# Last tile of the second feed-forward layer: eight single blocks and four pairs instead of two and seven, part of the tile before it kept in weight slots, and another hand-written order

## The chip, the cores and the metric

One core of one Trainium2 chip. The metric is the device time of one execution in microseconds (us), as a median over runs. Beside the runs there is one profiled execution, from which all rows below come; its times are counted from the first instruction's start (the span).

## What is computed

Attention with squared ReLU, gated by `u`, feeds two feed-forward layers. The change touches the second layer alone:

```python
# first layer (ELU), then the second one:
h = x @ w_in                                  # 6016 tokens, 256 -> 2048
P = a[0] + a[1]*h + a[2]*h*h + a[3]*h*h*h
Q = 1.0 + abs(b[0])*abs(h) + abs(b[1])*h*h
g = P / (Q + 1e-06)
out = g @ w_out                               # 2048 -> 256
```

## The kernel before

Everything is held transposed: features on partitions, tokens along the free dimension. Each fp32 matmul is done as three fp32r matmuls (high weight by high data, low weight by high data, high weight by low data), so every operand exists as a high and a low part. The 6016 tokens are cut into 12 tiles, eleven of 512 and a last one of 384. Below, tile 10 is the next to last (`NFT - 2`) and tile 11 the last (`NFT - 1`); "512" is a block of tile 10, "384" one block of tile 11 and "768" two blocks of tile 11 side by side (a pair, in two neighbouring PSUM banks).

The hidden features are 16 blocks of 128. For each block the first layer runs `first_hidden` (six matmuls), `first_relu` and `first_exp` on ScalarE, `first_elu` on VectorE, `first_high` on ScalarE, `first_low` on GpSimd and `project` (six matmuls). The second layer runs `second_hidden` (six matmuls into one PSUM bank, or twelve into two for a pair), then the twelve steps that `second` lists, then `second_project`. Tile 11's second layer starts only when all of tile 11's first layer is projected and `x2_high` (ScalarE) and `x2_low` (VectorE) have split its sum; this moment is called the hand-over below.

The steps of `second` have two forms. Tile 10 and the tiles before it take the plain one: `linear` and `size` on ScalarE read the block from PSUM, `denominator`, `times` and `numerator` on VectorE each read it from PSUM once more, then `absolute`, `log` and `power` on ScalarE, `high`, `product` and `remainder` on VectorE with both tensor inputs in SBUF, and `rest` on GpSimd. Tile 11 takes another: `square`, `size`, `linear` on ScalarE; `cubic` (p = p times s) on GpSimd; `denominator` on VectorE as q = s times b1 plus q, with both inputs in SBUF; no `absolute`; `numerator` (written over the block in PSUM), `high` and `remainder` on VectorE with one input in PSUM; `product` with both in SBUF; `rest` on GpSimd. `groups` says how tile 11's 16 blocks are grouped: one single, seven pairs, one single.

SBUF slots: `wide()` takes one of 32 slots which held the split weights. A slot comes free when its last reader has run: the first layer's weights as tile 11 passes through the first layer, the second layer's as it passes through the second. Tile 11's p, s, q, r sit in such slots. The high and low parts of tile 10's result sit in the three slots of tag `x` (`second`, step `high`).

Up to tile 10's first layer the order is that of `ffn_step`. The rest (`finish`) is an order written out by hand: the string `LAST` lists the operations two characters each, `ROOM` the PSUM bank of each that opens one; an operation goes to its engine's queue in the order listed, and each queue is in order. An operation beyond the list is `warm_up`, a matmul whose result nobody reads, to keep TensorE's clock up.

Of the kernel before, what the change touches and what calls it, by code (L numbers as in the profile page):

```python
# [21 lines left out]
def attention_then_two_ffns(  # L22
# [63 lines left out]
    def sb2(tag, bufs, dt=F32R):  # L86
        return sp.tile([P, 2, W], dt, tag=tag, bufs=bufs, name=tag)
# [68 lines left out]
    V = {}  # L156
# [309 lines left out]
        if d == ND - 1:  # L466
            give_pair(("acc", 0, ti))

    groups = [1] + [2] * 7 + [1]

    def members(i):

# [15 lines left out]
    def second(i):  # L488

        last = i[0] == NFT - 1
        st, m, n = mid[i], len(members(i)), widths[i[0]]
        h = st["h"]
        v, act, tt, stt = nc.vector, nc.scalar.activation, nc.gpsimd.tensor_tensor, nc.vector.scalar_tensor_tensor

        def new(key, tag, bufs, dt=F32):  # L500
            t = wide(dt) if last else sb(tag, bufs, dt).rearrange("p (c w) -> p c w", c=1)
            st[key] = t[:, :m, :n]
            return st[key]

        def linear():
            act(new("p", "t", 3), h, AF.Identity, bias=a2, scale=a3)  # L506

        def square():
            act(new("s", "", 0), h, AF.Square)

        def size():
            act(new("q", "q", 4), h, AF.Abs, scale=b0 if last else b1)  # L512

        def cubic():
            tt(out=st["p"], in0=st["p"], in1=st["s"], op=ALU.mult)

        def denominator():
            if last:
                stt(out=st["q"], in0=st["s"], scalar=b1, in1=st["q"], op0=ALU.mult, op1=ALU.add)
            else:  # L520
                stt(out=st["q"], in0=st["q"], scalar=b0, in1=h, op0=ALU.add, op1=ALU.mult)  # L521

        def times():
            v.tensor_tensor(out=st["p"], in0=st["p"], in1=h, op=ALU.mult)  # L524

        def numerator():
            if last:
                stt(out=h, in0=h, scalar=a1, in1=st["p"], op0=ALU.mult, op1=ALU.add)  # L528
                st["top"] = h
            else:  # L530
                stt(out=st["p"], in0=st["p"], scalar=a1, in1=h, op0=ALU.add, op1=ALU.mult)
                st["top"] = st["p"]

        def absolute():
            act(st["q"], st["q"], AF.Abs)

        def log():
            act(new("r", "r", 2), st["q"], AF.Ln, bias=NQ * LNS, scale=LNS)

        def power():  # L540
            act(st["r"], st["r"], AF.Exp, bias=LNB, scale=-1.0)

        def high():
            if last:
                tag, bufs = ("rl", 4) if i[1] % 2 else ("x", 3)
                st["hi"], st["lo"] = (sb2(tag, bufs)[:, :m, :n] for _ in range(2))
            else:
                t = sb2("x", 3)
                st["hi"], st["lo"] = t[:, 0:1, :n], t[:, 1:2, :n]
            stt(out=st["hi"], in0=st["top"], scalar=a0, in1=st["r"], op0=ALU.add, op1=ALU.mult)  # L550
            g2[i] = st["hi"], st["lo"]

        def product():
            st["prod"] = st["s" if last else "q"]
            stt(out=st["prod"], in0=st["q"], scalar=NQ, in1=f(st["hi"]), op0=ALU.add, op1=ALU.mult)  # L555

        def remainder():
            stt(out=st["p"], in0=st["top"], scalar=a0, in1=st["prod"], op0=ALU.add, op1=ALU.subtract)  # L558

        def rest():  # L560

            eng = v if i == (NFT - 1, len(groups) - 1) else nc.gpsimd
            eng.tensor_tensor(out=st["lo"], in0=st["p"], in1=st["r"], op=ALU.mult)  # L563

        reads = {"remainder"} if last else {"linear", "size", "denominator", "times", "numerator"}

        def then_free(name, fn):
            def run():
                fn()
                if name in reads:  # L570
                    reads.remove(name)
                    if not reads:
                        (give_pair if m > 1 else give)(("h", 1, i))
            return run

        if last:
            steps = [
                ("square", "A", ["hidden"], square),
                ("size", "A", ["hidden"], size),
                ("linear", "A", ["hidden"], linear),  # L580
                ("denominator", "V", ["square", "size"], denominator),
                ("cubic", "G", ["square", "linear"], cubic),
                ("log", "A", ["denominator"], log),
                ("power", "A", ["log"], power),
                ("numerator", "V", ["cubic", "size"], numerator),
                ("high", "V", ["power", "numerator"], high),
                ("product", "V", ["high"], product),
                ("remainder", "V", ["product"], remainder),
                ("rest", "G", ["remainder"], rest),
            ]  # L590
        else:
            steps = [
                ("linear", "A", ["hidden"], linear),
                ("size", "A", ["hidden"], size),
                ("denominator", "V", ["size"], denominator),
                ("times", "V", ["linear"], times),
                ("numerator", "V", ["times"], numerator),
                ("absolute", "A", ["denominator"], absolute),
                ("log", "A", ["absolute"], log),
                ("power", "A", ["log"], power),  # L600
                ("high", "V", ["power", "numerator"], high),
                ("product", "V", ["high"], product),
                ("remainder", "V", ["product"], remainder),
                ("rest", "G", ["remainder"], rest),
            ]
        return [(name, eng, needs, then_free(name, fn)) for name, eng, needs, fn in steps]

    def second_step(i, name):
        ops = mid[i].setdefault("ops", {x[0]: x[-1] for x in second(i)})
        ops[name]()  # L610

    def second_project(i, parts=("high", "low"), b=None):
        project(1, i[0], members(i), g2[i], parts, b)
# [44 lines left out]
    def ffn_step(n):  # L658
# [42 lines left out]
            second_hidden(j)  # L701

    DIGITS = "0123456789abcdefghijklmnopqrstuvwxyzABCDEFGHIJKLMNOPQRSTUVWXYZ_-"
    ROOM = "21303012610312103412301201320331203102602460260111111111111111111111111"
    LAST = (
        "590e0r0d1e1a0405060G1f0H0g1c0I0f000h075h0i020t1b0j5i08090k010K0J0u1d0L1h0l5j0a0s5k5a0x0m5l0V1g1i0v0n5p0w"
        "0y0o0X0Y0b5b035x1l0c1m5c0z0A0p1j1k5m5q0M0B0C0W5y0Z5d5r5z1n5A0q5s5e0N5f0-0_5F0D0E0O0P1p1q101C5G0Q11125g5H"
        "0R135t5I0T1o1R1r5u0S1E1F1t5B1s5C1T14151u1v0F5N5O1I1w1U5n5P5Q1x1D241G5o5J5v1J1y1S1z261H1K271X0U1L5V5W1Y1Z"
        "5K1V1W1M165D175w5L2j5R5T1_5S5X192l1N1O18611A5Y2m2562281-692a1P292k2p1B6a20632n642o2b2c2d6b6c2y2A1Q2B225E"
        "21232q2r2e2s6d6e5M2f2E2g2t2z2C2N6h2P2Q6i2D5Z5_6j2h6k2F2u2G6p2T5U302H2I2J2i2O2R2K5-6q6r326l6m333f6s2v2S60"  # L710
        "3h31342w2U3i653u352V2W6x673g3j662x2X2L686f363l3J2Y2M3k3w3x6y3m3n3o6z6A2Z6g6F373p38396B3v3A3q6C6n3L3a3y6N"
        "2_3M3r6t3b3c6O6P6Q3K3N6o3B3d3C2-3z3P3Y6G6H3O3Q3D6v4b3_3E6V3e3R6I3F3-4d4e3Z3s71423S3H3t6u6w3G4h3I403T3U3V"
        "4c4f724i416J4g6D73746K4j4k4344454q6E6W6X4F4l4s6R6S464m47754n6Y6L4U4r486M4t4H3W4W6Z4u4X766T4v4G4J4w3X4x4I"
        "4y4z4L4M6_6-6U4K7770494A784B7b4o4a4p7c794V7a4Y7d4N4O4C4_4-7g507e7i4Z4P514Q4R7f7s7t7v527x7h53544D4S7u7j4E"
        "4T7w7k7H7y7z7I7J7K7M7l5556587A577m7B7n7o7p7L7N7W7O7Z7Y7q7r7C7D7E7P7Q897R7X8b7_807-7S7T7F827G8o8183847U7V"
        "8a8d8c8e858q8D8f8g8h868i8j878m8p8s8r8F8t8k8l8w8u8v8x8E8G888I8H8J8K8S8U8T8B8y8z8A8n958V8X8L8M9m9m8C8N8W8Y"
        "8Q8O8P8_8Z8-97909698999b9c9m9m9m9m9m9m9m9m9m9m9m9m9m8R919a929d9e9f9g939m9m9m9m9m9m9i949h9m9m9m9j9k9l"
    )
    BACK = 1

# [3 lines left out]
    def finish(n0):  # L724
# [12 lines left out]
        for ti in range(NFT):  # L737
# [23 lines left out]
            for g in range(len(groups) if ti == tl else NF):  # L761
                i = ti, g
                b = (ti + 1) * NF + LAG1 + members(i)[0]
                if b + LAG2 < n0:
                    continue
                if b >= n0:
                    mid[i] = {"h": None}
                    add(lambda at, i=i: second_hidden(i, at), True)
                for name, *_ in second(i):
                    if b + lags[name] >= n0:  # L770
                        add(lambda i=i, name=name: second_step(i, name))
                add(lambda at=None, i=i: second_project(i, ("high",), at), g == 0)
                add(lambda i=i: second_project(i, ("low",)))
            if b + LAG2 >= n0:
# [147 lines left out]
```

## Time and profile before

| | us |
|---|---|
| median of 3 runs (lowest, highest) | 1544.7 (1544.42, 1545.58) |
| the profiled execution, its own time | 1544.23 |
| its span, first to last instruction | 1542.4 |
| VectorE's `elu` of tile 10's last block starts (first VectorE operation of `LAST`) | 1386.27 |
| tile 11's hand-over: its first `x2_low` starts | 1476.67 |
| VectorE's last operation but the copy of the result: `rest` of tile 11's last block ends | 1537.94 |

The page gives busy time by engine over the whole span; the span cut into stretches says which engine is full where. Durations of back-to-back operations overlap a little, so the distance from one start to the next is shorter than the duration.

### The profile page before, as it was taken

The numbers are of one execution on the slowest core, as the hardware profiler recorded it, in microseconds if no ns is written. First come the engines' busy times: TensorE is split into PE (matmuls) and PEld (weight loads), VectorE is DVE, ScalarE is ACT, GpSimd is POOL, SyncE is SP. The second block draws the span as 40 slices with busy tenths as digits, with TensorE's granted clock in tenths as the row PEclk, the third lists the DMA queues.
The fourth block names the chain that finished last, engine by engine and source line by source line (L and its number), as shares of the span: only waits on it lengthen the run. The fifth ranks groups of instructions, "written<-read, shape, count | busy, mean of one in ns | idle before, by whom it ended". The sixth has DMA issues, their size and how long they took to land.

```text
span 1542.4 us, 24205 instructions
## 1 busy us (share of the span) xinstructions
PE 1521.5 (99%) x8898; PEld 1292.8 (84%) x8898; DVE 1395.9 (90%) x1848; ACT 1290.3 (84%) x1996; POOL 679.9 (44%) x531
## 2 busy tenths in 40 slices
PE   9999999999999999999999999999999999999987
PEld 7889999898888878888888888888888888888866
DVE  8999999999996689999999999999999999999998
ACT  7878776787776798989899998989888998989974
POOL 3344430343342444444444444444444444445565
PEclk9999999999999999999999999999999999999999
DMA  5343333222222400000000000000000000000000
GB/s 150 124 130 117 111 120 109 64 76 68 83 81 83 135 1 1 28 1 28 1 0 29 1 28 1 28 1 27 2 1 28 1 25 1 14 1 15 1 14 11
DMA packets 38423, 67.09 MB, mean 43 GB/s; under 512 B 5408, under 2 KB 14880, under 8 KB 38304
## 3 DMA queue, kind: packets, MB, share of 16 engines
q1 hardware_dynamic: 38144, 65.29, 13.0%
q8 instruction: 69, 1.13, 0.3%
q14 instruction: 50, 0.41, 0.1%
q10 hardware_dynamic: 160, 0.26, 0.1%
HBM read 45.88 MB, written 19.66 MB: 42 GB/s over the span
## 4 chain that ended last, share of the span: by engine, by line
PE 58%; DVE 5%; issue 2%; POOL 1%; ACT 1%; POOLq 0%; DVEq 0%; ACTq 0%
PE psum L423 10%; PE psum L403 10%; PE psum L402 10%; PE psum L405 10%; PE psum L420 10%; PE psum L421 10%; POOL hl L454 1%; DVE w L555 1%; DVE x L550 1%; DVE t L558 1%; DVE psum L528 0%; DVE w L558 0%; DVE q L555 0%; DVE q L521 0%; DVE t L524 0%
## 5 line engine op out<-in xcount | busy, mean ns | idle before, releaser
L563 POOL TENSOR_TENSOR x<-t,r 128x512 fp32r<-128x512 f32 x176 | 231.5, 1315 | 478.0 <-DVE t L558 377.6
L329 PE MATMUL psum<-hl,w 64*128 64x512 f32 (+1 forms) x2256 | 392.4, 383 | 0.0
L329 PEld LDWEIGHTS psum<-hl,w 64*128 64x128 f32 x2256 | 306.0, 184 | 29.3 <-DVE e L350 1.8
L329 PE MATMUL psum<-x,w 64*128 64x512 f32 (+1 forms) x1128 | 319.2, 382 | 0.0
L454 POOL TENSOR_TENSOR hl<-e,hl 128x512 fp32r<-128x512 f32 (+1 forms) x192 | 248.2, 1293 | 67.2 <-ACT hl L449 60.7
L292 ACT ACTIVATE w<-psum 128x1024 f32<-128x1024 f32 (+1 forms) x144 | 145.2, 1009 | 102.5 <-PE psum L290 99.9
L329 PEld LDWEIGHTS psum<-x,w 64*128 64x128 f32 x1128 | 194.5, 184 | 13.4
L506 ACT ACTIVATE t<-psum,coef 128x512 f32<-128x512 f32 x176 | 137.4, 781 | 71.6 <-PE psum L405 69.6
L293 DVE SCALAR_TENSOR_TENSOR psum<-psum,w 128x1024 f32<-128x1024 f32 (+1 forms) x144 | 173.5, 1205 | 21.4 <-ACT w L292 20.8
L305 DVE TENSOR_TENSOR x<-psum,hl 128x1024 fp32r<-128x1024 f32 (+1 forms) x144 | 173.1, 1202 | 14.6 <-ACT q L205 0.5
L521 DVE SCALAR_TENSOR_TENSOR q<-q,coef,psum 128x512 f32<-128x512 f32 x176 | 131.2, 746 | 59.6 <-ACT q L512 59.4
L402 PE MATMUL psum<-x,w 128*128 128x512 f32 (+1 forms) x384 | 148.9, 388 | 7.2 <-DVE w L558 7.2
L298 ACT ACTIVATE hl<-w 128x1024 fp32r<-128x1024 f32 (+1 forms) x144 | 150.6, 1046 | 4.2
L420 PE MATMUL psum<-hl,w 128*128 128x512 f32 (+1 forms) x384 | 147.9, 385 | 0.4 <-ACT hl L449 0.4
L403 PE MATMUL psum<-x,w 128*128 128x512 f32 (+1 forms) x384 | 148.2, 386 | 0.0
L402 PE MATMUL psum<-rl,w 128*128 128x512 f32 (+1 forms) x384 | 148.1, 386 | 0.0
L403 PE MATMUL psum<-rl,w 128*128 128x512 f32 (+1 forms) x384 | 147.8, 385 | 0.0
L421 PE MATMUL psum<-hl,w 128*128 128x512 f32 (+1 forms) x384 | 147.7, 385 | 0.0
L442 DVE SCALAR_TENSOR_TENSOR e<-e,psum 128x512 f32<-128x512 f32 (+1 forms) x192 | 128.5, 670 | 17.7 <-ACT e L438 17.4
L420 PE MATMUL psum<-x,w 128*128 128x512 f32 (+1 forms) x368 | 142.9, 388 | 0.0
L421 PE MATMUL psum<-x,w 128*128 128x512 f32 (+1 forms) x368 | 142.8, 388 | 0.0
L558 DVE SCALAR_TENSOR_TENSOR t<-t,coef,q 128x512 f32<-128x512 f32 x176 | 136.8, 778 | 5.7
(137 smaller groups left out, 3518.6 us busy)
## 6 DMA issues: line engine op xcount, KB each, us to landing
raw<-w_in_dram SPq DMA_DIRECT2D x16, 512.0 KB, 4.2
raw<-w_out_dram SPq DMA_DIRECT2D x16, 512.0 KB, 4.6
wd<-q SPq DMA_DIRECT2D x28, 256.0 KB, 2.3
raw<-wd SPq DMA_DIRECT2D x14, 512.0 KB, 3.4
raw<-v_dram SPq DMA_DIRECT2D x22, 256.0 KB, 4.2
outT_dram<-raw SPq DMA_DIRECT2D x22, 256.0 KB, 2.5
raw<-uT_dram SPq DMA_DIRECT2D x10, 512.0 KB, 5.0
xd<-raw SPq DMA_DIRECT2D x20, 256.0 KB, 2.4
```

The lines of the kernel that those rows point to most:

```text
L293: nc.vector.scalar_tensor_tensor(out=s, in0=s, scalar=SCALE, in1=e, op0=ALU.mult, op1=ALU.mult)
L305: nc.vector.tensor_tensor(out=lo[:, :, :w], in0=psum[:, i:i + 2, :w], in1=f(hi[:, :, :w]), op=ALU.subtract)
L329: nc.tensor.matmul(acc[ti][d, h][:, :w], lhsT=lhs[rows, j % 2, d * P:(d + 1) * P], rhs=rhs[rows, :w], start=j == 0 and k == 0, stop=k == 2 ...
L402: nc.tensor.matmul(h, lhsT=wh[:, d, c], rhs=x[d][0], start=d == 0, stop=False)
L403: nc.tensor.matmul(h, lhsT=wl[:, d, c], rhs=x[d][0], start=False, stop=False)
L405: nc.tensor.matmul(h, lhsT=wh[:, d, c], rhs=x[d][1], start=False, stop=d == ND - 1)
L420: nc.tensor.matmul(out, lhsT=wh, rhs=g[0][:, c], start=k == 0, stop=False)
L421: nc.tensor.matmul(out, lhsT=wl, rhs=g[0][:, c], start=False, stop=False)
L423: nc.tensor.matmul(out, lhsT=wh, rhs=g[1][:, c], start=False, stop=k == NF - 1)
L454: nc.gpsimd.tensor_tensor(out=lo[:, 0], in0=e, in1=f(hi[:, 0]), op=ALU.subtract)
L558: stt(out=st["p"], in0=st["top"], scalar=a0, in1=st["prod"], op0=ALU.add, op1=ALU.subtract)
L563: eng.tensor_tensor(out=st["lo"], in0=st["p"], in1=st["r"], op=ALU.mult)
```

## The change

It groups tile 11's 16 blocks as one single, four pairs, seven singles, each with a form. "signed" (the pairs): `square` and `cubic` as before, but `denominator` is the plain one, (q plus b0) times h, reading the block from PSUM, and `absolute` is added on ScalarE. "banks" (the singles): as before, but ScalarE's `size` writes its result into a free PSUM bank, `denominator` reads and writes that bank, and `log` and `product` read it; `product` then gives the bank back. Tile 10's blocks 2 to 15 write their high and low parts into `wide()` slots instead of tag `x`. `ROOM` and `LAST` are replaced.

```diff
-    groups = [1] + [2] * 7 + [1]
+    LAYOUT = ((1, "banks"), (2, "signed"), (2, "signed"), (2, "signed"), (2, "signed"), (1, "banks"), (1, "banks"), (1, "banks"), (1, "banks"), (1, "banks"), (1, "banks"), (1, "banks"))
+    groups = [n for n, _ in LAYOUT]
+    KEPT = 2
+    def kept(i):
+        return i[0] == NFT - 2 and i[1] >= KEPT
...
+        squared = form in ("cubic", "signed", "banks")
+        signed = form not in ("cubic", "banks")
...
-        def size():
-            act(new("q", "q", 4), h, AF.Abs, scale=b0 if last else b1)
+        def size(b=None):
+            if form == "banks":
+                bank(("q", 1, i), b)
+                b = banks_of["q", 1, i]
+                st["q"] = psum[:, b:b + 1, :n]
+            else:
+                new("q", "q", 4)
+            act(st["q"], h, AF.Abs, scale=b1 if signed else b0)
...
         def denominator():
-            if last:
+            if signed:
+                stt(out=st["q"], in0=st["q"], scalar=b0, in1=h, op0=ALU.add, op1=ALU.mult)
+            else:
                 stt(out=st["q"], in0=st["s"], scalar=b1, in1=st["q"], op0=ALU.mult, op1=ALU.add)
...
-                t = sb2("x", 3)
+                t = wide() if kept(i) else sb2("x", 3)
...
+                if name == "product" and form == "banks":
+                    give(("q", 1, i))
...
+        if signed:
+            steps += [("absolute", "A", ["denominator"], absolute)]
```

What the two `LAST` strings spell, counted by engine. TensorE's are matmuls, the others' operations, by the free size of one; "to the hand-over" ends before `x2_high`, the rest is "after":

| | before, to it | after it | changed, to it | after it |
|---|---|---|---|---|
| TensorE 512 / 384 | 244 / 192 | 26 / 216 | 206 / 192 | 64 / 200 |
| of the 384, warm-ups | 0 | 24 | 0 | 8 |
| VectorE 512 / 768 / 384 | 118 / 0 / 16 | 8 / 35 / 14 | 109 / 0 / 16 | 17 / 20 / 44 |
| ScalarE 512 / 768 / 384 | 103 / 0 / 48 | 7 / 35 / 13 | 97 / 0 / 48 | 13 / 24 / 43 |
| GpSimd 512 / 768 / 384 | 19 / 0 / 16 | 3 / 14 / 3 | 18 / 0 / 16 | 4 / 8 / 15 |

VectorE's 384 after the hand-over hold two `x2_low` and the copy of the result in both.

## Rows read from the trace of the kernel before

**Rows 1.** The page: busy time, share and instructions of each engine
```profile
PE 1521.5 (99%) x8898; PEld 1292.8 (84%) x8898; DVE 1395.9 (90%) x1848; ACT 1290.3 (84%) x1996; POOL 679.9 (44%) x531
```
**Rows 2.** Stretches: length, busy PE, PEld, DVE, ACT, POOL (instructions), PE clock, DMA, GB/s
```profile
1360.00:1380.00 20.00, 20.00 (x90) 16.56 (x89) 18.74 (x29) 17.65 (x30) 9.82 (x8) 1.00 0.00 1
...
1400.00:1420.00 20.00, 20.00 (x100) 17.78 (x99) 19.61 (x31) 18.49 (x37) 11.72 (x9) 1.00 0.00 1
...
1480.00:1500.00 20.00, 14.50 (x73) 12.36 (x72) 19.60 (x19) 14.57 (x21) 14.29 (x8) 1.00 0.07 27
1500.00:1520.00 20.00, 17.07 (x87) 16.10 (x86) 19.62 (x17) 12.73 (x17) 11.87 (x7) 0.91 0.00 1
1520.00:1540.00 20.00, 14.23 (x67) 12.63 (x65) 17.91 (x18) 7.68 (x12) 9.50 (x6) 0.91 0.00 2
```
**Rows 3.** VectorE in order of time: start, duration, operation
```profile
1386.27 0.68 DVE L442 SCALAR_TENSOR_TENSOR e<-e,psum 128x512 f32<-128x512 f32 x1
...
1470.14 0.73 DVE L521 SCALAR_TENSOR_TENSOR q<-q,coef,psum 128x512 f32<-128x512 f32 x1
1470.80 0.67 DVE L524 TENSOR_TENSOR t<-t,psum 128x512 f32<-128x512 f32 x1
...
1476.67 1.02 DVE L465 TENSOR_TENSOR x<-psum,x 128x384 fp32r<-128x384 f32 x2
...
1484.78 2.34 DVE L558 SCALAR_TENSOR_TENSOR t<-t,coef,q 128x512 f32<-128x512 f32 x1
...
1491.45 0.62 DVE L558 SCALAR_TENSOR_TENSOR w<-psum,coef,w 128x384 f32<-128x384 f32 x1
1491.98 1.01 DVE L519 SCALAR_TENSOR_TENSOR w<-w,coef 128x768 f32<-128x768 f32 x1
...
1505.93 2.58 DVE L519 SCALAR_TENSOR_TENSOR w<-w,coef 128x768 f32<-128x768 f32 x1
1508.44 1.01 DVE L558 SCALAR_TENSOR_TENSOR w<-psum,coef,w 128x768 f32<-128x768 f32 x1
1509.37 1.01 DVE L528 SCALAR_TENSOR_TENSOR psum<-psum,coef,w 128x768 f32<-128x768 f32 x1
...
1531.04 0.96 DVE L555 SCALAR_TENSOR_TENSOR w<-w,rl 128x768 f32<-128x768 f32 x1
```
**Rows 4.** GpSimd in order of time, beside VectorE's row at 1505.93
```profile
1505.44 2.25 POOL L515 TENSOR_TENSOR w<-w 128x768 f32<-128x768 f32 x1 [0.49 <-ACT w L506]
```
**Rows 5.** By line and form, 1385 to 1543: busy, mean ns, idle before it
```profile
L519 DVE SCALAR_TENSOR_TENSOR w<-w,coef 128x768 f32<-128x768 f32 x7 | 10.2, 1460 | 0.0
L555 DVE SCALAR_TENSOR_TENSOR w<-w,rl 128x768 f32<-128x768 f32 x4 | 7.1, 1782 | 0.1
L555 DVE SCALAR_TENSOR_TENSOR w<-w,x 128x768 f32<-128x768 f32 x3 | 5.9, 1961 | 0.1
L519 DVE SCALAR_TENSOR_TENSOR w<-w,coef 128x384 f32<-128x384 f32 x2 | 3.0, 1489 | 0.0
L528 DVE SCALAR_TENSOR_TENSOR psum<-psum,coef,w 128x384 f32<-128x384 f32 x2 | 1.2, 611 | 0.0
L506 ACT ACTIVATE w<-psum,coef 128x384 f32<-128x384 f32 x2 | 1.3, 664 | 0.0
L509 ACT ACTIVATE w<-psum 128x384 f32<-128x384 f32 x2 | 1.0, 477 | 0.0
```
**Rows 6.** TensorE in order of time, at either clock
```profile
1533.32 0.52 PE L420 MATMUL psum<-rl,w 128*128 128x384 f32 x1
1533.64 0.52 PE L421 MATMUL psum<-rl,w 128*128 128x384 f32 x1
...
1536.11 0.33 PE L420 MATMUL psum<-x,w 128*128 128x384 f32 x1
1536.28 0.33 PE L421 MATMUL psum<-x,w 128*128 128x384 f32 x1
```
**Rows 7.** VectorE's waits from 1380 on: for whom, us in total, times, longest
```profile
DVE x L550 <- PE psum L423: 0.6, 1, 0.6
```

More of the change, by code (lines that the diff above doesn't have):

```diff
@@ L467, in x2_low, with form_of @@
             give_pair(("acc", 0, ti))
-    groups = [1] + [2] * 7 + [1]
+    LAYOUT = ((1, "banks"), (2, "signed"), (2, "signed"), (2, "signed"), (2, "signed"), (1, "banks"), (1, "banks"), (1, "banks"), (1, "banks"), (1, "banks"), (1, "banks"), (1, "banks"))
+    groups = [n for n, _ in LAYOUT]
+    KEPT = 2
+    BEFORE = "pppppppppppppppp"
+    def kept(i):
+        return i[0] == NFT - 2 and i[1] >= KEPT
+    def form_of(i):
+        if i[0] == NFT - 2:
+            return "banks" if BEFORE[i[1]] == "b" else "plain"
+        return LAYOUT[i[1]][1] if i[0] == NFT - 1 else "plain"
     def members(i):
@@ L488, in second @@
     def second(i):
-        last = i[0] == NFT - 1
+        last, form = i[0] == NFT - 1, form_of(i)
+        squared = form in ("cubic", "signed", "banks")
+        signed = form not in ("cubic", "banks")
         st, m, n = mid[i], len(members(i)), widths[i[0]]
@@ L508, in square @@
         def square():
-            act(new("s", "", 0), h, AF.Square)
-        def size():
-            act(new("q", "q", 4), h, AF.Abs, scale=b0 if last else b1)
+            act(new("s", "q", 4), h, AF.Square)
+        def size(b=None):
[6 more added lines that the diff above has]
+            act(st["q"], h, AF.Abs, scale=b1 if signed else b0)
         def cubic():
@@ L517, in denominator @@
         def denominator():
-            if last:
+            if signed:
+                stt(out=st["q"], in0=st["q"], scalar=b0, in1=h, op0=ALU.add, op1=ALU.mult)
+            else:
                 stt(out=st["q"], in0=st["s"], scalar=b1, in1=st["q"], op0=ALU.mult, op1=ALU.add)
-            else:
-                stt(out=st["q"], in0=st["q"], scalar=b0, in1=h, op0=ALU.add, op1=ALU.mult)
         def times():
@@ L526, in numerator @@
         def numerator():
-            if last:
-                stt(out=h, in0=h, scalar=a1, in1=st["p"], op0=ALU.mult, op1=ALU.add)
-                st["top"] = h
-            else:
-                stt(out=st["p"], in0=st["p"], scalar=a1, in1=h, op0=ALU.add, op1=ALU.mult)
-                st["top"] = st["p"]
+            st["top"] = st["p"] if form == "plain" else h
+            if squared:
+                stt(out=st["top"], in0=h, scalar=a1, in1=st["p"], op0=ALU.mult, op1=ALU.add)
+            else:
+                stt(out=st["top"], in0=st["p"], scalar=a1, in1=h, op0=ALU.add, op1=ALU.mult)
         def absolute():
@@ L553, in product @@
         def product():
-            st["prod"] = st["s" if last else "q"]
+            st["prod"] = st["s" if squared else "q"]
             stt(out=st["prod"], in0=st["q"], scalar=NQ, in1=f(st["hi"]), op0=ALU.add, op1=ALU.mult)
@@ L563, in rest, with run @@
             eng.tensor_tensor(out=st["lo"], in0=st["p"], in1=st["r"], op=ALU.mult)
-        reads = {"remainder"} if last else {"linear", "size", "denominator", "times", "numerator"}
+        reads = {"remainder"} if form != "plain" else {"linear", "size", "denominator", "times", "numerator"}
         def then_free(name, fn):
-            def run():
-                fn()
+            def run(*at):
+                fn(*at)
+                if name == "product" and form == "banks":
+                    give(("q", 1, i))
                 if name in reads:
@@ L574, in then_free @@
             return run
[L576 to L590, printed above, removed]
-        else:
[L592 to L605, printed above, removed]
@@ new lines, in second @@
+        steps = [("linear", "A", ["hidden"], linear), ("size", "A", ["hidden"], size)]
+        if squared:
+            steps += [("square", "A", ["hidden"], square), ("cubic", "G", ["square", "linear"], cubic)]
+        else:
+            steps += [("times", "V", ["linear"], times)]
+        steps += [
+            ("denominator", "V", ["size"] if signed else ["square", "size"], denominator),
+            ("numerator", "V", ["cubic" if squared else "times", *["size", "denominator"][:form != "plain" and 1 + signed]], numerator)]
@@ L606, in second, with second_step @@
+        if signed:
+            steps += [("absolute", "A", ["denominator"], absolute)]
+        steps += [
+            ("log", "A", ["absolute" if signed else "denominator"], log),
+            ("power", "A", ["log"], power),
+            ("high", "V", ["power", "numerator"], high),
+            ("product", "V", ["high"], product),
+            ("remainder", "V", ["product"], remainder),
+            ("rest", "G", ["remainder"], rest)]
         return [(name, eng, needs, then_free(name, fn)) for name, eng, needs, fn in steps]
-    def second_step(i, name):
+    def second_step(i, name, *at):
@@ L609, in second_step @@
         ops = mid[i].setdefault("ops", {x[0]: x[-1] for x in second(i)})
-        ops[name]()
+        ops[name](*at)
     def second_project(i, parts=("high", "low"), b=None):
@@ L703, in attention_then_two_ffns @@
     DIGITS = "0123456789abcdefghijklmnopqrstuvwxyzABCDEFGHIJKLMNOPQRSTUVWXYZ_-"
-    ROOM = "21303012610312103412301201320331203102602460260111111111111111111111111"
+    ROOM = "213203120623120321450314024030432353246524640123106713021336666666"
     LAST = (
[L706 to L717, printed above, removed]
@@ new lines, in attention_then_two_ffns @@
+        "1a04591e0d0f0h0r055a06075b5c08000e0g090a0t0G0H0I1b0K0i5h021f0j5i0J0v1g0k010L0l0m0s0u5d1c5p5q0M0n5e0w030o"
+        "5j5r5k5s1d0N0O0P0Q1h0V0X0x0R0b1i1l5l1j1k5m0p0y5x0W0c0z5F1m1n0Z0A0B5y0q5G5H0-5f1p5I0S0C105t0Y5z111C1r1D5g"
+        "0E0D1E0_1t5n5A1u121F135N1G141o1q5J5v1I1H5u5O5o151s0F5B5P5w5Q1R5V1v0T5K1J1w1x610U1y1z1S1T1V1U5C1K1L5W5X1X"
+        "5Y1W1M5R241Y16261Z1_1N1O1-625D255S632817182j2l2n192a275E5Z5_2b206429696a2y2A5L2C6b6c2c212d2e2k2N2E5M2f5T"
+        "2z6h6d5U6e6i2p656j2B2m2g2D2q305-2r3f6p6k2F2G3132606q3h2o2s2t2H662u2v6x6y34333j3u6l676m6r366s2I6z6A686F6f"
@@ new lines, in attention_then_two_ffns @@
+        "6t3g3l2J3w3i2K356N3m6u3k3y6O3n3o6P6Q3J6n6g37383p3K393L3q6B3r6v6G3a1A6H6o3N3M2P6I3b3c3O1P1B3P3Q3R226D3A2R"
+        "3Y3v6V3S3x6C3T3U3V6J6L3z2O6W2Q3B2T6X6Y2S3C3D2U6w2h2V2W6Z3_6E3E2w1Q4b232X3F3Z3-6K6M4d4f3G716R6S2Y7273742Z"
+        "4c4e414h4i4j4q4r6T6-6_4g2L4s40424k4t4l6U4u2i4F754344764m4n70454U4W4Y4w7778797a2_3d467b4H4x4G7c474v4y4I48"
+        "4z4J2x4A7d7s4_7g7f7i4V4X7e7h2M4B7j7v7t7w7u3s4Z7x7k7l7m2-4L4K4M3e7n7z7A7B3H4C3W3t3I7y7o7I7Y7C4N4O7D4-7K50"
+        "49517-7Z4o807_4P3X527E817L834a84854D4p7p8c7N7P8e7J4E53544Q4S55828687888h4R7Q4T7R567M57587q7r7O7S7F7T8s7U"
@@ L718, in attention_then_two_ffns @@
+        "8f8d8g8t8v8u8x8w7G7W8z8H7H8i8W8j7V7X8y8A8B8C8D8k8l8a8m8q8n898Z8Y8-8X8_8o8I908K8J918M928b8L938N998O94959a"
+        "9o8p8P8E8r9c9d9q8Q8R8F8U979r9t9p9s8G8S9b9e8T9u9v9w9f9D8V9x9g9S9h9G9i9y9j9k96989E9H9m9B9V9l9F9I9T9Wa79n9J"
+        "9U9X9z9A9K9L9Ma7a7a7a79Q9Y9C9Z9_9N9-a39Oa09Pa7a7a79Ra1a2a4a6a5"
     )
@@ L770, in finish @@
                     if b + lags[name] >= n0:
-                        add(lambda i=i, name=name: second_step(i, name))
+                        add(lambda *at, i=i, name=name: second_step(i, name, *at),
+                            name == "size" and form_of(i) == "banks")
                 add(lambda at=None, i=i: second_project(i, ("high",), at), g == 0)
```

## The prediction

> **What bounds the kernel now.** I read the page's busy times first, then the span in stretches, then VectorE's operations one by one with GpSimd's beside them, and last the operations grouped by form. The page says TensorE 99% [rows 1], and up to 1380 the stretches agree: TensorE 20.00 of 20.00, VectorE 18.74 [rows 2]. But the last stretches read otherwise: from 1480 TensorE is busy 14.50, 17.07 and 14.23 of 20 while VectorE has 19.60, 19.62 and 17.91 (it ends at 1537.94) [rows 2]. From 1400 on VectorE has 19.61 or more in each stretch shown but the last, so VectorE's queue sets the end from there, and TensorE waits for it after the hand-over at 1476.67. What the change is worth is therefore VectorE's time from 1386.27 to 1537.94, unless another engine takes over.
>
> The third view shows why VectorE is slow in tile 11. A `denominator` of 768 (L519) takes 1.01 us at 1491.98, and 2.58 us at 1505.93, where GpSimd's `cubic` runs from 1505.44 for 2.25 us [rows 3, 4]. Both inputs of that operation are in SBUF. The operations of that size with an input in PSUM take 1.01 us right behind it [rows 3]. Summed by form, seven L519 of 768 cost 10.2 us where 7 x 1.01 = 7.1 would do; two of 384 cost 3.0 where 2 x 0.62 = 1.2 would do; seven `product` of 768 (L555) cost 13.0 where 7 x 0.96 = 6.7 would do [rows 3, 5]. With the `remainder` of tile 10 at 1484.78 (2.34 for some 0.73, the price of its size without a neighbour) that is 3.1 + 1.8 + 6.3 + 1.6 = 12.8 us of VectorE lost beside GpSimd behind the hand-over [rows 3, 5].
>
> [...]
>
> **Part 1, up to the hand-over.** The new list places fewer operations before it: VectorE 109 of 512 instead of 118, with the same 16 of 384; TensorE 206 matmuls of 512 instead of 244. The old stretch is 1476.67 - 1386.27 = 90.4 us [rows 3]. Taking 0.47 for each `elu` of 384 (estimate: the 0.53 step of a 384 at 1491.45 [rows 3], and a little less), the 118 share 82.9 us, 0.70 each with their stalls included. Nine fewer: -6.3 us, hand-over near 1470.4. TensorE allows more: 38 x 0.222 (20 us by 90 instructions [rows 2]) = 8.4 us. ScalarE has six fewer; at 18.49 of 20 [rows 2] it is busy about 83.6 of 90.4 us, 0.55 for each of 151, so about 80.3 of the new 84.1 us, 95%. It still fits, with little to spare. What is moved isn't saved: it returns behind the hand-over.
>
> **Part 2, after the hand-over.** In steps from start to start: 0.53 for 384, 0.66 for 512, 0.93 for 768 (1491.45 to 1491.98, 1470.14 to 1470.80, 1508.44 to 1509.37 [rows 3]). Before: 35 x 0.93 + 8 x 0.66 + 13 x 0.53 = 44.7 us (the copy of the result lies behind the end); with 12.8 lost beside GpSimd that is 57.5 of the measured 61.3 us [rows 3, 5], so 3.8 us are small waits between dependent operations. After: 20 x 0.93 + 17 x 0.66 + 43 x 0.53 = 52.6 us. Of the 7.9 more, 9 x 0.66 = 5.9 came from part 1, and 2.0 is the fixed cost of more, smaller operations: three pairs become six singles, 15 more operations at 2 x 0.53 - 0.93 = 0.13. The small waits I scale by half with the groups (9 to 12), 4.5 us; all of it would be 5.1, none 3.8.
>
> What can still lose time beside GpSimd: the four `product` of the signed pairs, and 11 operations of tile 10 (three `high`, four `product`, four `remainder`) where there were six. The old `product` lost 6.3 / 7 = 0.9 us each [rows 5], the old six of tile 10 lost 1.6 / 6 = 0.27 each [rows 3]. I take 3.0 and 2.5, 5.5 us. The ends are 0 and 4 x 1.6 + 11 x 0.8 = 15 us (each loses as much as the worst row of its size: 2.58 for 0.96, and half of 1.6 [rows 3]). Then 52.6 + 4.5 + 5.5 = 62.6 us instead of 61.3: +1.3.
>
> The `denominator` and `product` of the singles work on PSUM. The nearest rows are L528 of 384, PSUM to PSUM, 0.611 us, and L558 of 384, PSUM to SBUF, 0.62, whose step to the next start is 0.53 [rows 3, 5]; I take 0.53 for all.
>
> [...]
>
> **ScalarE and GpSimd.** `size` into PSUM has no row; I bound it by ScalarE's 384 forms out of PSUM, 0.477 to 0.664 us [rows 5], so 8 x 0.19 = 1.5 us at most, and no loss on the path while ScalarE has room. The added work is four `absolute` of 768 and 15 more operations for the singles, about 4 x 0.9 + 15 x 0.2 = 6.6 us (estimates from 0.477 and 0.664 for 384 [rows 5] and the halves' fixed part). ScalarE is busy 12.73 and 7.68 of 20 in the last stretches [rows 2], and that hides it there; without that cover its price would be these 6.6 us. GpSimd has 15 + 8 + 4 operations instead of 3 + 14 + 3. At 1.3, 2.0 and 1.4 us (estimates from 2.25 for 768 [rows 4]) that is 41 of 61 us, up from 36: room, but more neighbours for VectorE.
>
> **The kept slots.** `high` writes elsewhere at the same size: 0. Counted along the new list, the free weight slots never fall below three (seven before), and around the hand-over they are reused soon after `second_project` of tile 10 has read them. `high` of blocks 14 and 15 on VectorE would then wait for TensorE, with tile 11's `product`s queued behind. One such wait for a matmul in the old trace is 0.6 us [rows 7]: 0 to 1.2 us; I take 0, since TensorE's list has those reads far ahead.
>
> **TensorE.** After the hand-over 64 x 0.222 + 200 x 0.17 (1536.11 to 1536.28 [rows 6]) = 48.2 of 62.6 us, more even than before. The work now standing behind the hand-over fills its holes.
>
> **Sum.** -6.3 + 1.3 = -5.0 us. Against the profiled execution's 1544.23 that is 1539.2; the median lay 0.5 above it, so 1539.7. What lies behind VectorE's last operation (two matmuls, copies, transfers) is the same.
>
> **Rivals.** (a) *GpSimd is dodged throughout*: nothing is lost, -10.5: 1534.2. For it: losses happen only where an operation with two SBUF inputs falls beside GpSimd, and few of these are left. Against: GpSimd is busier at the end. (b) *The gain is handed on*: ScalarE at 95% before the hand-over stalls VectorE, or the 15 sensitive operations lose what the old ones lost (12.8 instead of 5.5, +7.3 - 5.0 = +2.3); about 1543 to 1547. (c) *Slower by the clock*: the last list has 8 warm-ups instead of 24, and the granted clock was 0.91 in the last stretches even with them [rows 2]. [...] After tile 10's last projection 146 matmuls of 384 are left; VectorE has then some 36 x 0.53 + 8 x 0.93 + 5 = 31.5 us. [...] Against: the holes before it are now filled. (d) *The list doesn't do what it says*, a wait that I don't see in the hand-over, up to no change: counted with (b).
>
> [...]
>
> **Chances.** Forecast 0.53 (1536 to 1542), (a) 0.13, (b) 0.24, (c) 0.10. A measurement tells about 0.2%, 3.1 us: faster is under 1541.6, slower over 1547.8. Faster: 0.13 + 0.50 + 0.04 of (b) = 0.67; same 0.22; slower 0.11. The range reaches from (a) and the case of no loss, 1533.5, to nearly the whole of (b), 1546.0.
>
> **What would show it.** Part 1: the first `x2_low` starts near 1470 instead of 1476.67. Part 2: L519 is gone as an SBUF-only group and the singles' `denominator` and `product` stay near 0.6 us; only signed `product`s show 2 us and more. TensorE's busy share from 1480 rises. Wrong would be: VectorE showing waits for ScalarE or TensorE behind the hand-over, matmuls of 0.52 in long rows, or `remainder`s of tile 10 above 1.4 us in number.

## The result

The changed kernel takes 1530.17 us (median of 4 runs, 1529.79 to 1530.58) against 1544.7: 14.5 us less, a ratio of 0.9905 with a 95% interval from 0.9888 to 0.9922. The forecast was 1539.7 with a range from 1533.5 to 1546.0. The direction is right, the size is nearly three times what was forecast, and the time lies below the range. The profiled execution took 1529.85 us with a span of 1528.1.

The stretches of the changed kernel (length, busy PE, PEld, DVE, ACT, POOL, PE clock, DMA, GB/s):

```profile
1400.00:1420.00 20.00, 20.00 (x100) 17.85 (x99) 19.34 (x31) 19.32 (x39) 9.49 (x8) 1.00 0.00 1
...
1480.00:1500.00 20.00, 17.34 (x85) 15.03 (x86) 19.65 (x22) 16.13 (x24) 13.30 (x9) 1.00 0.07 27
1500.00:1520.00 20.00, 18.90 (x102) 17.37 (x103) 19.40 (x34) 17.62 (x35) 16.51 (x14) 1.00 0.00 1
```

VectorE is as full as before, 19.40 to 19.65 of 20, so its queue is still what sets the end. What differs is TensorE beside it: 17.34 and 18.90 busy where it had 14.50 and 17.07, with a granted clock of 1.00 where it had 0.91 in the second of them [rows 2]. ScalarE is at 19.32 in the stretch from 1400, some 97% where the forecast had 95%, and VectorE still has 19.34 there.

VectorE in order of time in the changed kernel, the lines that answer to [rows 3]:

```profile
1386.52 0.68 DVE L442 SCALAR_TENSOR_TENSOR e<-e,psum 128x512 f32<-128x512 f32 x1
...
1467.99 0.55 DVE L465 TENSOR_TENSOR x<-psum,x 128x384 fp32r<-128x384 f32 x1
...
1496.25 2.50 DVE L574 SCALAR_TENSOR_TENSOR w<-w,x 128x768 f32<-128x768 f32 x1
...
1522.91 0.56 DVE L582 TENSOR_TENSOR rl<-w 128x384 fp32r<-128x384 f32 x1
```

From the first `elu` of the list to the first `x2_low` it is 81.5 us instead of 90.4 (-8.9); from there to the end of the last `rest` (1523.47) it is 55.5 instead of 61.3 (-5.8). Together -14.7 us. The list starts 0.25 us later in this execution, so VectorE's last `rest` ends 14.5 us earlier (1523.47 instead of 1537.94), which is the result.

VectorE by line and form from 1375 on (busy, mean ns, idle before), the lines that answer to [rows 5]:

```profile
L577 DVE SCALAR_TENSOR_TENSOR t<-t,coef,q 128x512 f32<-128x512 f32 x24 | 18.2, 761 | 0.2
L541 DVE SCALAR_TENSOR_TENSOR psum<-w,coef,psum 128x384 f32<-128x384 f32 x8 | 4.9, 614 | 0.1
L539 DVE SCALAR_TENSOR_TENSOR w<-w,coef,psum 128x768 f32<-128x768 f32 x4 | 3.9, 1004 | 0.0
L574 DVE SCALAR_TENSOR_TENSOR w<-w,x 128x768 f32<-128x768 f32 x2 | 3.5, 1728 | 0.1
L574 DVE SCALAR_TENSOR_TENSOR w<-psum,rl 128x384 f32<-128x384 f32 x4 | 2.2, 549 | 0.0
L574 DVE SCALAR_TENSOR_TENSOR w<-w,rl 128x768 f32<-128x768 f32 x2 | 2.1, 1046 | 0.0
```

The `denominator`s (L541, L539) and the singles' `product`s (L574 of 384; the four that read `x` in place of `rl` take 548) cost their price without a neighbour: 614, 1004 and 549 ns. One signed `product` of four is long, the 2.50 us at 1496.25. And in tile 10 the `remainder` (L577, 512) has a mean of 761 ns; the line of the same operation before, over the same part of the list, reads

```profile
L558 DVE SCALAR_TENSOR_TENSOR t<-t,coef,q 128x512 f32<-128x512 f32 x24 | 22.5, 941 | 0.3
```

so 4.3 us of the gain lie in operations of tile 10 whose form the change doesn't touch (1.9 of them in front of the hand-over, 2.4 behind it).

### The profile page after: what moved, and what is told of

Same layout as the page of the kernel before. It is cut to its first block, busy times and chain, and to the rows that moved or that the text cites. A ratio compares the mean times of both kernels' runs of the same rounds, so it can differ in the third digit from the quotient of the medians.

```text
span 1528.1 us, 24221 instructions
## 1 busy us (share of the span) xinstructions
PE 1515.9 (99%) x8882; PEld 1298.3 (85%) x8882; DVE 1381.3 (90%) x1863; ACT 1294.9 (85%) x2015; POOL 678.9 (44%) x537
## 4 chain that ended last, share of the span: by engine, by line
PE 89%; DVE 4%; issue 2%; POOL 2%; ACT 2%; DMA 1%; POOLq 0%; SPq 0%; DVEq 0%; ACTq 0%
PE psum L329 23%; PE psum L402 10%; PE psum L405 10%; PE psum L403 10%; PE psum L423 10%; PE psum L420 10%; PE psum L421 10%; PE psum L290 6%; POOL hl L454 1%; DVE psum L293 1%; DVE w L574 0%; DVE x L305 0%; DVE w L577 0%; DMA q<-zT_dram 0%; POOL w L582 0%
## 5 line engine op out<-in xcount | busy, mean ns | idle before, releaser
L582 POOL TENSOR_TENSOR x<-t,r 128x512 fp32r<-128x512 f32 x162 | 211.1, 1303 | 460.7 <-DVE t L577 363.2
L329 PE MATMUL psum<-hl,w 64*128 64x512 f32 (+1 forms) x2256 | 397.6, 383 | 0.0
L329 PE MATMUL psum<-x,w 64*128 64x512 f32 (+1 forms) x1128 | 324.0, 382 | 0.0
L292 ACT ACTIVATE w<-psum 128x1024 f32<-128x1024 f32 (+1 forms) x144 | 145.2, 1009 | 102.8 <-PE psum L290 101.2
L329 PEld LDWEIGHTS psum<-x,w 64*128 64x128 f32 x1128 | 190.7, 184 | 10.5
L539 DVE SCALAR_TENSOR_TENSOR q<-q,coef,psum 128x512 f32<-128x512 f32 x176 | 131.5, 747 | 60.0 <-ACT q L532 59.8
L402 PE MATMUL psum<-x,w 128*128 128x512 f32 (+1 forms) x384 | 148.4, 386 | 2.1 <-DVE w L577 2.0
L403 PE MATMUL psum<-x,w 128*128 128x512 f32 (+1 forms) x384 | 147.8, 385 | 0.0
L577 DVE SCALAR_TENSOR_TENSOR t<-t,coef,q 128x512 f32<-128x512 f32 x176 | 132.5, 753 | 5.6
L551 DVE SCALAR_TENSOR_TENSOR t<-t,coef,psum 128x512 f32<-128x512 f32 x176 | 131.2, 747 | 5.6
L420 PE MATMUL psum<-x,w 128*128 128x512 f32 (+1 forms) x340 | 131.9, 388 | 1.1 <-DVE w L577 0.7
```

Of the source, the lines that this page charges most:

```text
L329: nc.tensor.matmul(acc[ti][d, h][:, :w], lhsT=lhs[rows, j % 2, d * P:(d + 1) * P], rhs=rhs[rows, :w], start=j == 0 and k == 0, stop=k == 2 ...
L402: nc.tensor.matmul(h, lhsT=wh[:, d, c], rhs=x[d][0], start=d == 0, stop=False)
L403: nc.tensor.matmul(h, lhsT=wl[:, d, c], rhs=x[d][0], start=False, stop=False)
L420: nc.tensor.matmul(out, lhsT=wh, rhs=g[0][:, c], start=k == 0, stop=False)
```

## The experiments

Three readings were to be told apart. **A**: VectorE's queue is the end, and the gain is time that it no longer loses beside GpSimd. **B**: the gain comes from tile 10's projections, which now stand behind the hand-over on TensorE. **C**: the list and the grouping gain it, whatever the forms. Ratios are to the kernel before on the same chip, with a 95% interval. Microseconds against the changed kernel compare medians from different chips, on which the kernel before took 1544.6 to 1545.2 us; by the intervals, two changed versions are told apart at some 3.5 us, and a smaller difference rests on the rows that are shown with it.

### The kernel before without the cubic

```diff
         def cubic():
-            tt(out=st["p"], in0=st["p"], in1=st["s"], op=ALU.mult)
+            pass
```

> The kernel before with tile 11's cubic on GpSimd left out (its numerator then lacks the product of linear and square); all else and the order as before. Theory A (VectorE's queue is the end, and what it loses beside GpSimd is the time to be had): six of the long operations of tile 11 (2.4 to 2.6 us instead of 1.0) start beside a cubic, so some 9 to 11 us go: 1534 to 1536. Theory B (the gain comes from tile 10's projections standing behind the hand-over, which this kernel doesn't have): VectorE's lost time was hidden behind TensorE, within 2 us of 1544.7.

Measured: 1532.79 us, ratio 0.9923 (0.9907 to 0.9940), 11.8 us less, with VectorE's and TensorE's lists untouched. By form, from 1385 on:

```profile
L519 DVE SCALAR_TENSOR_TENSOR w<-w,coef 128x768 f32<-128x768 f32 x7 | 7.1, 1010 | 0.0
L555 DVE SCALAR_TENSOR_TENSOR w<-w,rl 128x768 f32<-128x768 f32 x4 | 4.6, 1159 | 0.1
L555 DVE SCALAR_TENSOR_TENSOR w<-w,x 128x768 f32<-128x768 f32 x3 | 2.9, 958 | 0.1
L558 DVE SCALAR_TENSOR_TENSOR t<-t,coef,q 128x512 f32<-128x512 f32 x22 | 18.6, 849 | 0.2
```

The seven `denominator`s of 768 fall from 10.2 to 7.1 us, the seven `product`s from 13.0 to 7.5 [rows 5]: 8.6 us of the 11.8. Another 2.4 are in tile 10's `remainder`, 21.0 us before over the same window. VectorE had no wait for GpSimd in the kernel before, so what went is time inside its operations. B is excluded as the whole reason, since this list has none of the moved projections. TensorE had the room: the old kernel's end was VectorE's queue, and GpSimd's `cubic` made it long.

### The kernel before with signed denominators, and with the kept slots

```diff
         def size():
-            act(new("q", "q", 4), h, AF.Abs, scale=b0 if last else b1)
+            act(new("q", "q", 4), h, AF.Abs, scale=b1)
...
         def denominator():
-            if last:
-                stt(out=st["q"], in0=st["s"], scalar=b1, in1=st["q"], op0=ALU.mult, op1=ALU.add)
-            else:
-                stt(out=st["q"], in0=st["q"], scalar=b0, in1=h, op0=ALU.add, op1=ALU.mult)
+            stt(out=st["q"], in0=st["q"], scalar=b0, in1=h, op0=ALU.add, op1=ALU.mult)
...
         def log():
+            if last:
+                act(st["q"], st["q"], AF.Abs)
```

> The kernel before, order unchanged, with the signed denominator for all nine groups of tile 11 (it reads the block from PSUM; the log step is preceded by an absolute on ScalarE). Theory A: the nine denominators lost 3.1 + 1.8 = 4.9 us beside GpSimd and lose none now; 4 to 5 us faster, 1540, less what nine more ScalarE operations (7 x 0.8 + 2 x 0.5 = 6.6 us) put on the path from denominator to high. Theory B: 1544.7, or slower by the longer path. A third way: the loss isn't gone but moves to the next operation with two SBUF inputs, the product: 1543 to 1545.

Measured: 1541.62 us, ratio 0.9981 (0.9972 to 0.9991), 3.0 us less. By form, and with the idle time in front of each:

```profile
L525 DVE SCALAR_TENSOR_TENSOR psum<-psum,coef,w 128x768 f32<-128x768 f32 x7 | 7.1, 1020 | 4.4 <-POOL w L515 4.4
...
L518 DVE SCALAR_TENSOR_TENSOR w<-w,coef,psum 128x768 f32<-128x768 f32 x7 | 7.1, 1009 | 0.8 <-ACT w L506 0.8
L554 DVE SCALAR_TENSOR_TENSOR w<-w,rl 128x768 f32<-128x768 f32 x4 | 5.5, 1366 | 0.1
L549 DVE SCALAR_TENSOR_TENSOR rl<-psum,coef,w 128x768 fp32r<-128x768 f32 x4 | 4.1, 1018 | 2.3 <-ACT w L540 2.3
```

The lost time goes as A says: L518 has 1009 ns each, and the seven `product`s of 768 take 8.4 us instead of 13.0, so the loss didn't move to them as the third way has it. But some 7 us come back as waits in the old order: `numerator` 4.4 us for GpSimd's `cubic`, `high` 2.3 for ScalarE's `power`, whose chain has one operation more. In this order the form by itself is worth 3.0 us; the waits leave room for an order that has something else for VectorE to do there.

```diff
-                t = sb2("x", 3)
+                t = wide() if i[0] == NFT - 2 and i[1] >= 2 else sb2("x", 3)
```

> The kernel before, order unchanged, with tile 10's blocks 2 to 15 written to weight slots instead of tag x. Both theories: the order already fits three slots, so no operation starts earlier or later by more than tenths: 1544.7 within 1. If the slots themselves freed VectorE of waits, 1 to 2 us faster (VectorE's waits in the old trace add up to some 2 us there).

Measured: 1544.79 us, ratio 1.0001 (0.9991 to 1.0010). The slots alone do nothing. The changed list needs them: `high` of tile 10's blocks 2 to 15 stands in front of the projections that would give the three slots of tag `x` back. The changed list without them was therefore not tried.

### The changed kernel with the old forms

The singles' `size` in a weight slot again:

```diff
-            if form == "banks":
-                bank(("q", 1, i), b)
-                b = banks_of["q", 1, i]
-                st["q"] = psum[:, b:b + 1, :n]
-            else:
-                new("q", "q", 4)
+            new("q", "q", 4)
...
-                if name == "product" and form == "banks":
-                    give(("q", 1, i))
```

> The changed kernel, order unchanged, with the eight singles' size in a weight slot instead of a PSUM bank, so that their denominator and product have two SBUF inputs again. Theory A: GpSimd is busy 16.5 of 20 us there; in the old trace such an operation of 384 lost 0.9 us (denominator) and 0.3 (product): 8 x 0.9 + 8 x 0.3 = 9.6 us, half to all of it, 1535 to 1540. Theory C (the order and its placing is what gains; the form doesn't matter): within 1 us of 1530.2.

Measured: 1537.35 us, ratio 0.9951 (0.9935 to 0.9968), 7.2 us more than the changed kernel. The singles' `denominator`s now read

```profile
L536 DVE SCALAR_TENSOR_TENSOR w<-w,coef 128x384 f32<-128x384 f32 x8 | 8.9, 1110 | 0.0
```

which is 4.0 us more than 4.9. The singles' `product`s take 1.4 us more and tile 10's `remainder` 1.0 (mean 804 ns instead of 761): 6.4 of the 7.2.

The pairs' denominators in the old form (in `LAST`, `square` of pair 4 also moves in front of that pair's `denominator`, which now needs it):

```diff
-    LAYOUT = ((1, "banks"), (2, "signed"), (2, "signed"), (2, "signed"), (2, "signed"), ...
+    LAYOUT = ((1, "banks"), (2, "cubic"), (2, "cubic"), (2, "cubic"), (2, "cubic"), ...
...
-        if signed:
-            steps += [("absolute", "A", ["denominator"], absolute)]
+        if signed or form == "cubic":
+            steps += [("absolute", "A", ["denominator"], absolute if signed else lambda: None)]
```

> The changed kernel with the four pairs' denominators in the old form (two SBUF inputs, no absolute; square of pair 4 moved in front of its denominator). Theory A: four denominators of 768 that can lose 0 to 1.6 us each, 0.45 on average in the old trace: +2 (0 to 6). Theory C: unchanged or up to 1 us faster, as ScalarE is rid of four operations of 0.85 us.

Measured: 1533.51 us, ratio 0.9926 (0.9911 to 0.9941), 3.3 us more, of which 2.5 in

```profile
L541 DVE SCALAR_TENSOR_TENSOR w<-w,coef 128x768 f32<-128x768 f32 x4 | 6.4, 1629 | 0.0
```

Both together:

> Both: no form of tile 11 is changed, only grouping, kept slots and order. Theory A: the two losses add, +7 to +14, 1537 to 1544: the order alone is worth 1 to 8 us of the 14.5. Theory C: within 1 us of 1530.2, the order is worth all of it.

Measured: 1538.61 us, ratio 0.9959 (0.9944 to 0.9974), 8.4 us more. `denominator` (L536) by form in this last one:

```profile
L536 DVE SCALAR_TENSOR_TENSOR w<-w,coef 128x384 f32<-128x384 f32 x8 | 7.4, 928 | 0.0
L536 DVE SCALAR_TENSOR_TENSOR w<-w,coef 128x768 f32<-128x768 f32 x4 | 6.0, 1524 | 0.0
```

Against 614 and 1004 ns in the changed kernel these two lines lose 2.5 and 2.1 us, and the singles' `product`s (850 and 837 ns against 549) another 2.4. So both A and C have a part: of the 14.5 us the new forms make 8.4 with this list, and list, grouping and slots together about 6; these three were not separated. The two forms don't add (7.2 + 3.3 is more than 8.4): the eight L536 of 384 lose 2.5 us here and 4.0 when they alone are in the old form. Why they lose less here no run shows; that a late VectorE operation also shifts GpSimd's next one would fit.

The hand-over says where each part lies. In this run VectorE's list starts at 1387.03, and the first `x2_low` and the last `rest` read

```profile
1468.48 0.55 DVE L465 TENSOR_TENSOR x<-psum,x 128x384 fp32r<-128x384 f32 x1
...
1531.52 0.56 DVE L577 TENSOR_TENSOR rl<-w 128x384 fp32r<-128x384 f32 x1
```

To the hand-over that is 81.5 us, as in the changed kernel, so the whole 8.9 us of that part come without the new forms. Behind it it is 63.6 us, 2.3 more than the kernel before and 8.1 more than the changed kernel: the forms act behind the hand-over alone.

### The changed kernel with the projections in front of the hand-over

```diff
  TensorE's list (11.15 is block 15 of tile 11; the first layer's there, the second's elsewhere)
-  project 11.15, split, project 10.6-10.10 high and 10.4-10.10 low, second_hidden 11.0 ...
+  project 10.6-10.10 high and 10.4-10.10 low, project 11.15, split, second_hidden 11.0 ...
```

> The changed kernel with 34 of tile 10's projection matmuls put back in front of the hand-over on TensorE (20 of blocks 6 to 10 high, 14 of blocks 4 to 10 low), nothing else moved: 34 x 0.222 = 7.5 us more TensorE work before the hand-over. If the hand-over's place is needed, x2_low comes up to 6 us later, VectorE's queue stands still behind it, and the time is 4 to 7 us longer (1534 to 1537). If VectorE has cover, less than 2 us.

Measured: 1538.29 us, ratio 0.9956 (0.9941 to 0.9971), 8.1 us more, above the 4 to 7 expected. VectorE at the hand-over:

```profile
1476.02 0.56 DVE L465 TENSOR_TENSOR x<-psum,x 128x384 fp32r<-128x384 f32 x1 [7.10 <-ACT x L460]
```

The 34 matmuls are 7.5 us, and VectorE stands still for 7.10 of them; `x2_low` comes 8.0 us later than in the changed kernel, as VectorE is 0.9 us later from the list's start on in this execution. There is next to no cover: in the changed kernel ScalarE's split in front of `x2_low` waits 0.2 us for TensorE, so VectorE and TensorE reach the hand-over together. Moving the projections isn't a gain by itself (they have to be done anyway); it is what lets VectorE's shorter list end earlier.

### What is left in the changed kernel

```diff
         def cubic():
-            tt(out=st["p"], in0=st["p"], in1=st["s"], op=ALU.mult)
+            pass
```

> The changed kernel with tile 11's cubic on GpSimd left out (its numerator lacks the product of linear and square). Theory A says that almost all that VectorE could lose beside GpSimd is gone already: two product of 768 lose 1.8 us together, one of them beside a cubic (2.50 us at 1496.25 against 0.96), so 1528 to 1530, where the same cut gave 11.8 us on the kernel before. If more than 4 us go, losses or waits for GpSimd are left that the rows by form don't show.

Measured: 1528.77 us, 1.4 less than the changed kernel, where the same cut took 11.8 us from the kernel before. That is nearly all that the one long `product` loses (2.50 - 0.96 = 1.5), and in this run it takes 0.96 us as the other of its form does.

> The changed kernel without its 8 warm-up matmuls. If TensorE's clock is held up by the matmuls that now stand behind the hand-over, granted clock 1.00 but for the last few us and 1530 to 1531. If the 8 warm-ups hold it, the last stretch falls to 0.9 or less, matmuls of 384 step by 0.32 instead of 0.17 us there and the time is 1 to 3 us longer.

(edit: the eight `warm_up` entries are taken out of the list.) Measured: 1529.84 us (1529.69 to 1530.02), no different from the changed kernel. The granted clock in the stretch from 1520 is 0.87 instead of 0.94, too late to matter; from 1480 to 1520 it is 1.00 without them.

One try to get the last 1.5 us: the long `product` moved out of the cubic's way.

```diff
  VectorE's list
-  denominator 11.4, numerator 11.2, high 11.2, product 11.2, remainder 11.2
+  numerator 11.2, high 11.2, product 11.2, denominator 11.4, remainder 11.2
```

> The changed kernel with one operation moved on VectorE: the denominator of pair 4 behind the product of pair 2 instead of ahead of its numerator. The product then starts about 0.9 us earlier, beside the end of a rest instead of the start of a cubic (GpSimd 1493.84 to 1495.69, then 1496.09). Theory A: it loses some 0.4 instead of 1.5 us: about 1 us faster, 1529.1. Rival: GpSimd's cubic moves up with it, or the log of pair 4 comes late and VectorE waits for it: 1530.2 or up to 1 us slower.

Measured: 1532.8 us, ratio 0.9922 (0.9907 to 0.9936), 2.6 more than the changed kernel: slower as the rival says, by more than it says, and by a wait that it doesn't name. The `product` is down to 0.96 us. But these waits are new (who waits for whom: us in total, times, longest), of ScalarE and of VectorE:

```profile
ACT w L523 <- DVE w L539: 3.8, 1, 3.8
```
```profile
DVE psum L541 <- ACT psum L532: 2.3, 1, 2.3
```

ScalarE's `square` of pair 4 (L523) stands behind that pair's `denominator` (L539) in the list and now waits 3.8 us for it, although neither needs the other's result. Both read the same PSUM block; whether that is why, no run shows. ScalarE's queue behind it brings the next single's `size` late, and VectorE waits 2.3 us. Moving `square` too was not tried. A version faster than the changed kernel by more than the measurement can tell was not found.

## Why the prediction was wrong

**What held.** VectorE's queue as the end, the loss beside GpSimd as what there is to gain (the kernel before without `cubic`: 11.8 us, forecast 12.8 lost behind the hand-over in all), the steps of 0.53, 0.66 and 0.93 us, no price for PSUM operands (614 ns for the singles' `denominator`, where [rows 5] had 611 for L528), no loss on ScalarE, no price for the slots, and against the rival of the clock: 1.00 until 1520, with or without warm-ups (in the kernel before the granted clock was 0.50 from 1532.00 to 1534.50, where the matmuls of [rows 6] step by 0.32; the 0.10 for that rival was my estimate, and no run shows time lost by it). Two readings of rows are off without weight in the sum: the stretch from 1480 has 19.60, not "19.61 or more", and 2.58 is a `denominator` with a price of 1.01, not 0.96. What failed are three terms of the sum.

**Part 1, -6.3 forecast, -8.9 measured.** The nine operations fewer are 9 x 0.66 = 5.9 us. I had charged every remaining operation with the old mean of 0.70, its losses beside GpSimd included, as if those went with the operation and not with the order. They didn't stay. VectorE's `remainder` by form between the list's start and the hand-over, first before, then changed:

```profile
L558 DVE SCALAR_TENSOR_TENSOR t<-t,coef,q 128x512 f32<-128x512 f32 x20 | 17.1, 861 | 0.2
```
```profile
L577 DVE SCALAR_TENSOR_TENSOR t<-t,coef,q 128x512 f32<-128x512 f32 x18 | 13.8, 766 | 0.2
```

Over a price of 740 ns (0.73 us for the 512 at 1470.14 [rows 3]) that is a loss of 2.4 us before and 0.5 after. Tile 10's `high` (over 740 ns) and `product` (over 680) lose some 2.1 us before and 0.9 after. Together 3.2 us less, which with the 5.9 makes 9.1, near the 8.9. I had this term in none of the rivals, so even (a), "GpSimd is dodged throughout", came out at 1534.2.

**Part 2, losses, 5.5 us forecast, 1.9 measured.** The four signed `product`s lose 5.6 - 4 x 0.96 = 1.8 instead of 3.0, and tile 10's eleven operations 0.1 instead of 2.5. A rate from the old order (0.27 us for each sensitive operation) was carried to the new one, although there GpSimd's operations stand at other places. The old rates fail for the old forms in the new list too: there the eight L536 of 384 lose 0.3 us each and the four of 768 0.5, where the old rows had 0.9 and 0.45.

**Part 2, small waits, 4.5 us forecast, 1.0 measured** (55.5 less 52.6 of steps and 1.9 of losses). The 3.8 us that I took from the old trace were a remainder, and part of it was loss that I hadn't listed: a second `remainder` of tile 10,

```profile
1481.20 1.51 DVE L558 SCALAR_TENSOR_TENSOR t<-t,coef,q 128x512 f32<-128x512 f32 x1
```

0.8 us over its price, and 0.6 of a `product` of 384 (1.14 us at 1535.49). The other 2.4 us are, row by row, gaps where an operation stands directly behind the one whose result it needs: in the old list `high` to `product` of one pair is 1.05 us from start to start where 0.93 is the step, and `numerator` to `high` 1.11 (1509.37 to 1510.48).

```profile
1510.48 1.02 DVE L550 SCALAR_TENSOR_TENSOR x<-psum,coef,w 128x768 fp32r<-128x768 f32 x1
1511.53 0.96 DVE L555 SCALAR_TENSOR_TENSOR w<-w,x 128x768 f32<-128x768 f32 x1
```

Scaling the remainder up with the number of groups was the wrong way: where the changed list puts two singles side by side, another block's operation stands between, and the step is 0.52.

```profile
1514.14 0.61 DVE L569 SCALAR_TENSOR_TENSOR rl<-psum,coef,w 128x384 fp32r<-128x384 f32 x1
1514.67 0.61 DVE L569 SCALAR_TENSOR_TENSOR x<-psum,coef,w 128x384 fp32r<-128x384 f32 x1
1515.19 0.55 DVE L574 SCALAR_TENSOR_TENSOR w<-psum,rl 128x384 f32<-128x384 f32 x1
```

Where a single's `high` and `product` do follow each other, at 1510.40 and 1511.04, it is 0.64.

**The sum.** -6.3 + 1.3 should have been -8.9 - 5.8: 2.6 us from part 1, 3.6 from the losses and 3.5 from the small waits, all three of one kind. Each was a loss or a gap of the old order, taken over as a price of the operation. Rival (a), dodging GpSimd throughout, was the nearest, at 0.13, and nearly what happened; its 1534.2 kept the old losses of part 1 and the gaps. The range failed for the same reason: its low end let the loss behind the hand-over go to nothing, but kept the one in front of it and the small waits.

**Hand-over.** The forecast had VectorE late at the hand-over (1470.4) and TensorE some 2 us ahead. It came at 1467.99, where TensorE and VectorE meet; the moved projections were needed almost whole (7.10 us of waiting when 7.5 us of them were put back).

## What to carry to other kernels

An operation of VectorE with two SBUF inputs can cost more than twice its price (2.58 us for 1.01, 2.34 for 0.73) where it starts while a GpSimd operation runs, so in a stretch that VectorE bounds, giving it one PSUM input (another form of the same formula, or an intermediate that ScalarE leaves in a free bank) can be worth more than removing an operation (a `denominator` of 768 took 2.58 us before and the four signed ones 1.00 each, where the step of one is 0.93). When pricing a new order, price each operation without its neighbours and give the losses a term of their own, which can go to zero in every stretch that is reordered; what a remainder of "small waits" holds should be looked up before it is scaled. A new form pays more with an order that fills the waits it opens: the signed form in the old order gained 3.0 us, and 8.4 us of the result hang on the forms with the new list.

## What the runs showed of the hardware

ScalarE writing `size` into PSUM takes the middle of the bounds, 0.564 us, where a `size` of 384 into SBUF took 0.570 in the kernel before, and `log` out of PSUM is no slower (0.492, against 0.524 out of SBUF before); by form in the changed kernel behind the hand-over:

```profile
L532 ACT ACTIVATE psum<-psum,coef 128x384 f32<-128x384 f32 x8 | 4.5, 564 | 0.4 <-PE psum L731 0.4
L557 ACT ACTIVATE w<-psum 128x384 f32<-128x384 f32 x8 | 3.9, 492 | 4.1 <-DVE psum L541 4.0
```

On VectorE, the singles' `product` takes 549 ns with a PSUM input, and without one and without a neighbour it took before

```profile
1490.87 0.54 DVE L555 SCALAR_TENSOR_TENSOR w<-w,x 128x384 f32<-128x384 f32 x1
```

so the PSUM input costs it 0.01 us, nothing that this kernel can feel.

GpSimd busy 16.51 of 20 us (1500 to 1520) took nothing from VectorE as long as VectorE's operations there had a PSUM operand: 19.40 busy, all forms at their price (means of 550 to 617 ns for 384, 1009 to 1021 for 768). With GpSimd at 11.87 in that stretch before [rows 2], three operations begun in it took 2.58, 2.60 and 2.61 us (1505.93, 1512.41 and 1518.84): each has two SBUF inputs and starts while a GpSimd operation runs. In these rows the one that starts first loses nothing. In the kernel before, this `product` began 0.39 us ahead of the `cubic` at 1505.44 [rows 4] and kept its price:

```profile
1505.05 0.96 DVE L555 SCALAR_TENSOR_TENSOR w<-w,rl 128x768 f32<-128x768 f32 x1
```

The `cubic` took 2.25 us instead of 1.84, the shortest of its size there, and the `denominator` begun at 1505.93, while the `cubic` ran, the 2.58 us of [rows 3]. In the changed kernel a `product` of 768 at 1504.85 does the same to the two `cubic`s from 1505.17 on: 0.96 us itself, 2.49 for the two of them, which take 1.0 each further on.
